# Wider DMA rows, a new order of the output stores and a new placement of the zero stores in a decode forward-and-backward kernel

## The chip, the cores and the metric

The kernel runs on one core of one Trainium2 chip. The metric is the device time of one launch in microseconds. It was measured five times for the kernel before, and one further execution was profiled. All engine names are those of the profile: PE is the matrix engine, DVE and ACT are the two engines that copy results out of PSUM, POOL and SP issue transfers (SP does nothing else).

## The reference

A single token passes through four residual layers, attention (A1), MLP (B2), attention (A3), MLP (B4), and the kernel returns the output and the gradients of everything. The two attentions share their weights and caches, and so do the two MLPs, so every weight gradient is a sum over two layers.

```python
x = x + A(layernorm(x), k_cache, v_cache, wq, wo)   # 32 heads over 4 KV heads, last 4096 of 32768 positions
x = x + B(layernorm(x), w1, b1, w2)                 # h*tanh(softplus(h)), width 3584
x = x + A(layernorm(x), k_cache, v_cache, wq, wo)
x = x + B(layernorm(x), w1, b1, w2)
# results: x, and the vjp with grad_out for x, k_cache, v_cache, wq, wo, w1, b1, w2
```

All tensors are bfloat16 and D is 1024. The gradients of k_cache and v_cache have all 32768 positions, of which the first 28672 are zero. These zeros alone are 58.7 MB of the 98.8 MB that the kernel writes. The weight gradients are outer products of one column with one row per layer, so they cost almost no arithmetic and a lot of copying and storing.

## The kernel before

**Order of the work.** The program is one straight sequence: A1 forward (`attn_fwd`), B2 forward (`mlp_fwd`), A3 forward, then `mlp_turn`, which does B4 forward and the W1 part of its backward in seven blocks of 512 columns, then A3 backward (`attn_bwd`), the second pass over W2 (`W2Pass.rest`, which serves B4's forward and B2's backward), `mlp_bwd_w1` for B2, A1 backward, and at last a list of `jobs` that makes and stores the weight gradients. K, V, wq and ten of sixteen pieces of wo stay in the core's memory. The rest of wo, W1 and W2 stream through six slots (`strm`, `NB = 6`), so a load is issued by SP when the piece six before it has been used up.

**Loads.** SP first loads K (four transfers of 1 MB), wq (sixteen of 512 KB, lines 444 to 446: eight row blocks `t`, two halves each, so 4 KB per partition), V, and wo. `w1_block` (line 705) loads a block of W1 for B4 as 1 KB rows.

**Zero stores.** There are 112 zero stores of 512 KB. `bg_zeros(n, after)` (line 134) lets POOL issue n of them once the tile `after` has been written: a tiny copy to `gate_t` waits for it. `zeros(n)` (line 128) lets SP issue them. The table `Z` (line 1143) says how many go where: `A3` in A3 forward, `B4[b]` ahead of the loads of B4's block b, `A3c` and `A3d` in A3 backward, `B4w` in the W2 pass, `W1` and `W1m` in `mlp_bwd_w1` (one for each listed i), `A1c` on POOL in A1 backward. `A1d=100` lets SP issue all that are left there: 27.

**Output jobs.** A job makes 2048 columns of a gradient (1792 for W1) in four PSUM banks, DVE and ACT copy 1024 each to the core's memory (`ev_out`), and SP stores them. `stage["w"]` holds 14 jobs for dW2 and 16 for dW1 (`dw_wide`), `stage["v"]` 8 for dV and `stage["k"]` 8 for dK (`dkv`), `stage["o"]` 16 for dWo and `stage["q"]` 16 for dWq. Jobs of w, o and q store 512 KB each (dW1 448 KB) from slots of a rotating list. The dV and dK jobs fill the memory of `kv["K"]` and store twice, after jobs 3 and 7, in 4 KB rows. `weave(a, b)` puts one job of b after every two of a. The order is 14 dW2, then dW1 with dV, then dWo with dK, then dWq. Ten small preparation jobs (`late_prep`: layouts for later jobs) are put in at every fourth place from the fifth on. After the jobs nothing is left but the stores in flight.

Of the kernel before, what the change touches and what calls it, by code (L numbers as in the profile page):

```python
# [14 lines left out]
P = 128  # L15
HQ = 32
DH = 128
G = 4
# [5 lines left out]
def kernel(  # L24
# [22 lines left out]
    nc = tc.nc  # L47
# [5 lines left out]
    J = A_wq.shape[1]  # L53
# [11 lines left out]
    NW2 = TF // 2  # L65
# [19 lines left out]
    wq_v = A_wq.rearrange("(t p) j -> p t j", p=P)  # L85
# [48 lines left out]
    def bg_zeros(n, after):  # L134

        if n:
            nc.gpsimd.tensor_copy(gate_t[:], after[:, 0:1])
        for _ in range(min(n, len(zero_jobs))):
            nc.gpsimd.dma_start(zero_jobs.pop(0), zt[:])  # L139
# [18 lines left out]
    def shaped(t, shape):  # L158
        n = 1
        for k in shape[1:]:  # L160
            n *= k
        ap = t[0:shape[0], 0:n]
        if len(shape) == 3:
            return ap.rearrange("p (a b) -> p a b", a=shape[1])
        if len(shape) == 4:
            return ap.rearrange("p (a b c) -> p a b c", a=shape[1], b=shape[2])
        return ap
# [63 lines left out]
    def mm(out_ap, lhsT, rhs, start, stop, **kw):  # L231
        nc.tensor.matmul(out_ap, lhsT=lhsT, rhs=rhs, start=start, stop=stop, skip_group_check=True, **kw)  # L232
# [48 lines left out]
    def level():  # L281
        ev[:] = [0.0, 0.0]
# [50 lines left out]
    wq_b = keep.tile([P, TD, 2, J // 2], BF16, name="wq_b")  # L333
    wq_t = [wq_b[:, t, hf, :] for t in range(TD) for hf in range(2)]
# [4 lines left out]
    def load_kv(pool, nm, src):  # L339
        kv[nm] = pool.tile([P, G, TK, DH], BF16, name=nm)  # L340
        for g in range(G):
            nc.sync.dma_start(kv[nm][:, g, :, :], src[g])

    def kv_units(nm):
        for g in range(G):
            f = kv[nm][:, g, :, :].rearrange("p t d -> p (t d)")
            for k in range(4):
                yield f[:, k * 1024:(k + 1) * 1024]

    def wo_load(c):  # L350
        if c < NR:
            w = wo_kept[c]
        else:
            w = strm.tile([P, 2, D], BF16, name="wo_c", tag="st")[:]
        nc.sync.dma_start(w, wo_v[c])
        return w
# [30 lines left out]
    def pipe(items, T, M, lag=1):  # L387
        n = len(items)
        for i in range(n + lag):
            if i < n:  # L390
                T(items[i])
            if i >= lag:
                M(items[i - lag], i - lag)

    area = {}
# [44 lines left out]
    def attn_fwd(x_col, lname, first):  # L440
        if first:
            load_kv(keep, "K", k_v)
            ku = list(kv_units("K"))
            for t in range(TD):
                for hf in range(2):
                    nc.sync.dma_start(wq_t[2 * t + hf], wq_v[:, t, hf * (J // 2):(hf + 1) * (J // 2)])
            load_kv(keep, "V", v_v)
            for c in range(NR):
                wo_load(c)
# [22 lines left out]
        if not first:  # L472
            for c in range(NR, min(NO, NR + NB)):
                held[c] = wo_load(c)
            bg_zeros(Z["A3"], n_bf)
            for w in wq_t:
# [74 lines left out]
        for i, c in enumerate(order):  # L551
            if c not in held and c not in early:
                held[c] = wo_load(c)
            w = wo_kept[c] if c < NR else held.pop(c)
# [113 lines left out]
    def mlp_fwd(x_col, lname, g_bf):  # L668
# [5 lines left out]
        for i in range(2 * TD):  # L674
            t, hf = i // 2, i % 2
            w = w1_load(i)
            if i == 0:
                bg_zeros(Z["B2a"], x_col)
            if i == 4:
# [17 lines left out]
        sv["dact"] = dact  # L697
        x_new, wg = w2.rest(0, g_bf, x_col, f"x_{lname}", gbc, Z["B2"], last)
        return x_new, sv, wg
# [5 lines left out]
    def w1_block(b, hh):  # L705
        w = strm.tile([P, HT, CB], BF16, name="w1_b", tag="st")
        nc.sync.dma_start(w[:], w1_v[:, hh * HT:(hh + 1) * HT, b * CB:(b + 1) * CB])
        return w

    def mlp_turn(x_col, lname, wg, g_col, nxt):  # L710
# [22 lines left out]
        def lo0(b):  # L733
            return max(b - 1, 0) * FB
# [6 lines left out]
        for b in range(NBK):  # L741
            bg_zeros(Z["B4"][b], dh_bf[:, lo0(b):] if b else n_bf)
            ws[b] = [w1_block(b, hh) for hh in range(2)]
# [38 lines left out]
    def mlp_bwd_w1(g_col, lname, sv, nxt):  # L782
# [3 lines left out]
        def T(i):  # L786
            w = w1_load(i)
            ws[i] = w
            if i in Z["W1m"]:
                bg_zeros(1, ws[i - 1])  # L790
# [9 lines left out]
        level()  # L800
        bg_zeros(Z["W1"], sv["dh_bf"])
        pipe(list(range(2 * TD)), T, M)
# [229 lines left out]
    def stage_tile(shape):  # L1032
        s = slots.pop(0)
        slots.append(s)
        return shaped(s, shape)

    def ev_out(out_ap, in_ap, f=1.0):
        evac(out_ap, in_ap, 1.22 * f, 1.05 * f)

    def outer(lhsT, rhs, q, ps):  # L1040
        mm(ps, lhsT, rhs, True, True, tile_position=(32 * q, 0))

    jobs = []
# [5 lines left out]
    def out_banks():  # L1049

        if "pair" in pools:
            ts = [pools["pair"].tile([P, 1024], FP32, name="ops", tag="pair") for _ in range(2)]
            return [t[:, k * 512:(k + 1) * 512] for t in ts for k in range(2)], [(0, 2, ts[0][:]), (2, 2, ts[1][:])]
        bs = [psum1([P, 512], FP32, "ops") for _ in range(4)]
        return bs, [(k, 1, bs[k]) for k in range(4)]
# [13 lines left out]

        jobs.extend([lambda c=c: chunk(c) for c in range(nblk // 2)])  # L1070

    def dw_wide(R, last, step, perm, out_t):

        def chunk(t, hf):
            st = stage_tile([P, 2048])
            bs, gs = out_banks()
            for q in (0, 1, 2, 3):
                n = 512 if q < 3 else last
                outer(R()[32 * q:32 * q + 2, 0, t * P:(t + 1) * P], R()[32 * q:32 * q + 2, 1, hf * 512:hf * 512 + n], q, bs[q][:, 0:n])
            for k, n, ap in gs:  # L1080
                w = min(n * 512, step - k * 512)
                o, i = st[:, k * 512:k * 512 + w], ap[:, 0:w]
                if perm:
                    o, i = o.rearrange("p (c x t) -> p c t x", x=P, t=2), i.rearrange("p (c t x) -> p c t x", x=P, t=2)
                ev_out(o, i, w / 1024)
            nc.sync.dma_start(out_t[t * P:(t + 1) * P, hf * step:(hf + 1) * step], st[:, 0:step])

        jobs.extend([lambda t=t, hf=hf: chunk(t, hf) for t in range(TD) for hf in range(2)])

    def dkv(x3, y3, x1, y1, out_t):  # L1090
        ov = out_t[0, :, Sk - W:, :].rearrange("g (p t) d -> p g t d", p=P)

        def chunk(j):
            st = kv["K"]
            bs, gs = out_banks()
            for lay, (x, y) in enumerate(((x3, y3), (x1, y1))):
                for c in range(NC):
                    mm(bs[c], x[32 * c:32 * c + 32, j * P:(j + 1) * P],
                       y[32 * c:32 * c + 32, :, :].rearrange("p g d -> p (g d)"), lay == 0, lay == 1, tile_position=(32 * c, 0))
            for k, n, ap in gs:  # L1100
                t0 = 4 * j + k
                ev_out(st[:, :, t0:t0 + n, :].rearrange("p g t d -> p t g d"), ap.rearrange("p (t g d) -> p t g d", t=n, g=G), n / 2)
            if j % 4 == 3:
                for g in range(0, G, 2):
                    hs = slice(4 * j - 12, 4 * j + 4)
                    nc.sync.dma_start(ov[:, g:g + 2, hs, :], st[:, g:g + 2, hs, :])

        jobs.extend([lambda j=j: chunk(j) for j in range(TJ)])

# [30 lines left out]
        for _ in range(min(n, len(prep))):  # L1140
            prep.pop(0)()

    Z = dict(B2a=1, B2={0: 1, 4: 1, NW2 - 2: 3}, A3=16, B4=[4, 2, 2, 2, 2, 2, 5], A3c=6, A3d=27, B4w={1: 1, 4: 1, 7: 1, 10: 1}, W1=2, W1m=(5, 10), A1c=3, A1d=100)


    x1 = None
# [35 lines left out]
    x1, sA1 = attn_fwd(x0, "A1", True)  # L1182
    x2, sB2, wg4 = mlp_fwd(x1, "B2", gcolb)
    x3, sA3 = attn_fwd(x2, "A3", False)
# [46 lines left out]
    def r3(nm):  # L1231
        return area[nm].rearrange("p (g d) -> p g d", g=G)

    slots.extend(wq_t)
    stage = {}

    def take(nm):
# [1 line left out]
        del jobs[:]  # L1239

    take("w")
    dkv(area["p3"], r3("do3"), sA1["p"], r3("do1"), out_3)
    take("v")
    dw_tall("wo", HQ, out_5.rearrange("(c p t) d -> c p t d", p=P, t=2))
    take("o")
    dkv(sA3["ds"], r3("q3"), sA1["ds"], r3("q1"), out_2)
    take("k")
    dw_wide(lambda: area["Rq"], 512, 2048, False, out_4)
    take("q")
    late_prep = [  # L1250
        lambda: row_layout(sA3["dorep"], "do3"),
        lambda: row_layout(sA1["dorep"], "do1"),
        lambda: tall_left("wo", "o", 0),
        lambda: tall_left("wo", "o", 1),
        lambda: tall_right("wo", "gA"),
        lambda: row_layout(sA3["qrep"], "q3"),
        lambda: row_layout(sA1["qrep"], "q1"),
        lambda: rows_put(area["Rq"], 0, "nA", "rep"),
# [1 line left out]
        db1_out,  # L1260
    ]

    def weave(a, b):
        while a or b:
            jobs.extend(a[0:2])
            jobs.extend(b[0:1])
            del a[0:2], b[0:1]

    n2 = NW2
    jobs.extend(stage["w"][:n2])  # L1270
    weave(stage["w"][n2:], stage["v"])
    weave(stage["o"], stage["k"])
    jobs.extend(stage["q"])
    for k, f in enumerate(late_prep):
        jobs.insert(5 + 4 * k, f)
    run(1000)
    zeros(1000)
    assert not zero_jobs
# [30 lines left out]
```

## Time and profile before

| what | value |
|---|---|
| median of five runs | 447.18 us (443.79 to 449.1) |
| the profiled execution, whole | 445.38 us |
| its span | 443.6 us |
| bytes moved | 171.18 MB, mean 386 GB/s |
| packets | 52048, of which 1076 of 8 KB or more |
| busy: PE, DVE, ACT, POOL | 73%, 54%, 50%, 14% |
| zero stores: on POOL, on SP | 85, 27 |

The profiled execution took 1.8 us less than the median. Of its 445.38 us, 1.78 lie outside the span. The busy shares of the engines are means over stages that differ a lot. The share that is even over the whole span is that of the transfers, so this page is read from its DMA rows, and then stage by stage.

### The profile page before, as it was taken

The numbers are of one execution on the slowest core, as the hardware profiler recorded it, in microseconds if no ns is written. First come the engines' busy times: TensorE is split into PE (matmuls) and PEld (weight loads), VectorE is DVE, ScalarE is ACT, GpSimd is POOL, SyncE is SP. The second block draws the span as 40 slices with busy tenths as digits, with TensorE's granted clock in tenths as the row PEclk, the third lists the DMA queues.
The fourth block names the chain that finished last, engine by engine and source line by source line (L and its number), as shares of the span: only waits on it lengthen the run. The fifth ranks groups of instructions, "written<-read, shape, count | busy, mean of one in ns | idle before, by whom it ended". The sixth has DMA issues, their size and how long they took to land.

```text
span 443.6 us, 11728 instructions
## 1 busy us (share of the span) xinstructions
PE 323.4 (73%) x5004; PEld 218.4 (49%) x5004; DVE 240.6 (54%) x492; ACT 220.8 (50%) x256; POOL 63.9 (14%) x165
## 2 busy tenths in 40 slices
PE   1466756498988699887899588878966777888930
PEld 0233515397376699775596577856422212122100
DVE  2134201196343367665374664465359788999950
ACT  1121200065144377766693354435037777998940
POOL 2000000011332122242142112014010100000000
PEclk9998655575888889989999758998975555555555
DMA  8999999999999989999999999999999969899997
GB/s 317 377 413 418 406 409 385 409 384 378 392 415 380 395 298 369 402 410 387 417 414 407 353 383 348 381 400 414 417 417 407 417 253 396 331 406 405 404 405 315
DMA packets 52048, 171.18 MB, mean 386 GB/s; under 512 B 5184, under 2 KB 12380, under 8 KB 50972
## 3 DMA queue, kind: packets, MB, share of 16 engines
q1 hardware_dynamic: 39536, 125.58, 73.0%
q0 software_dynamic: 12416, 44.84, 25.6%
q8 instruction: 39, 0.64, 0.6%
q14 instruction: 13, 0.11, 0.1%
q10 hardware_dynamic: 44, 0.01, 0.0%
HBM read 71.58 MB, written 98.84 MB: 384 GB/s over the span
## 4 chain that ended last, share of the span: by engine, by line
PE 22%; ACT 13%; DMA 7%; DVE 6%; issue 3%; POOL 1%; DVEq 0%; ACTq 0%; SPq 0%
DMA w_c<-in_B_w_dram 7%; PE tps L196 6%; PE ops L232 5%; ACT wq_b L149 5%; PE acc L232 4%; ACT K L149 2%; PE sm L232 2%; ACT wo_b L149 2%; ACT st_o L149 2%; ACT V L149 2%; PE rw L983 2%; DVE K L146 1%; PE d L232 1%; PE tps L630 1%; DVE st_o L146 1%
## 5 line engine op out<-in xcount | busy, mean ns | idle before, releaser
L139 POOL DMA_DIRECT2D out_dram<-zt x85 | 45.5, 538 | 42.4 <-DMA out_dram<-zt 37.3
L232 PEld LDWEIGHTS <-w_c 128*128 128x128 bf16 x1120 | 37.4, 102 | 23.3 <-DMA w_c<-in_B_w_dram 17.6
L640 ACT COPY w_c<-tps 128x1024 bf16<-128x1024 bf16 x28 | 28.3, 1012 | 28.6 <-PE tps L630 20.9
L654 DVE CUSTOM_DVE_ANT_0 scr<-w_c,gbc 128x1024 bf16<-128x1024 bf16 x28 | 34.2, 1221 | 10.6 <-DMA w_c<-in_B_w_dram 9.3
L232 PE MATMUL ops<-V 2*128 2x512 bf16 (+1 forms) x160 | 34.2, 600 | 5.0 <-DVE K L146 2.7
L232 PEld LDWEIGHTS <-V 128*128 128x128 bf16 (+2 forms) x448 | 17.1, 102 | 37.5 <-issue 37.2
L149 ACT CAST wq_b<-ops 128x1024 bf16<-128x1024 f32 (+1 forms) x32 | 33.4, 1120 | 3.8 <-PE ops L232 3.4
L149 ACT COPY K<-tps 128x1024 bf16<-128x1024 bf16 x20 | 19.6, 1021 | 29.6 <-PE tps L196 29.5
L146 DVE CAST wq_b<-ops 128x1024 bf16<-128x1024 f32 (+1 forms) x28 | 30.5, 1144 | 1.1 <-PE ops L232 1.0
L232 PE MATMUL ops<-wo_b 2*128 2x512 bf16 x120 | 23.7, 571 | 8.0 <-ACT wo_b L149 2.3
L630 PE MATMUL tps<-ident_bf,w_c 128*128 128x128 bf16 x224 | 23.9, 273 | 0.7 <-DMA w_c<-in_B_w_dram 0.7
L232 PE MATMUL q<-wq_b,nA_pair 128*32 128x512 bf16 x128 | 10.8, 418 | 16.8 <-DMA wq_b<-in_A_wq_dram 16.8
L146 DVE CAST K<-ops 128x1024 bf16<-128x1024 f32 x16 | 19.6, 1224 | 6.2 <-PE ops L232 6.1
L149 ACT COPY w_b<-tps 128x1024 bf16<-128x1024 bf16 x20 | 19.5, 1015 | 6.1 <-PE tps L196 4.7
L232 PE MATMUL acc<-a_pair,w_c 128*128 128x16 bf16 x448 | 15.9, 173 | 8.4 <-DMA w_c<-in_B_w_dram 8.3
L146 DVE COPY K<-tps 128x1024 bf16<-128x1024 bf16 x12 | 8.1, 690 | 25.5 <-PE tps L196 23.6
L248 DVE COPY yr<-acc 128x512 f32<-128x512 f32 x6 | 4.2, 692 | 30.2 <-PE acc L232 30.2
L196 PE MATMUL tps<-ident_bf,K 128*128 128x128 bf16 x256 | 19.3, 235 | 0.0
L196 PE MATMUL tps<-ident_bf,w_c 128*128 128x128 bf16 x224 | 16.5, 231 | 3.1 <-DMA w_c<-in_B_w_dram 2.9
L630 PEld LDWEIGHTS <-w_c 128*128 128x128 bf16 x224 | 18.1, 123 | 1.2 <-DMA w_c<-in_B_w_dram 0.8
L149 ACT CAST K<-ops 128x1024 bf16<-128x1024 f32 x16 | 16.2, 1012 | 5.1 <-PE ops L232 5.0
L149 ACT COPY w_c<-tps 128x768 bf16<-128x768 bf16 (+1 forms) x14 | 11.6, 830 | 14.0 <-PE tps L196 14.0
(326 smaller groups left out, 655.5 us busy)
## 6 DMA issues: line engine op xcount, KB each, us to landing
out_dram<-zt POOLq DMA_DIRECT2D x85, 512.0 KB, 10.2
w_c<-in_B_w_dram SPq DMA_DIRECT2D x32, 448.0 KB, 6.3
w_c<-in_B_w_dram SPq DMA_DIRECT2D x28, 512.0 KB, 7.1
out_dram<-zt SPq DMA_DIRECT2D x27, 512.0 KB, 10.1
wo_c<-in_A_wo_dram SPq DMA_DIRECT2D x24, 512.0 KB, 7.3
wq_b<-in_A_wq_dram SPq DMA_DIRECT2D x16, 512.0 KB, 11.5
out_dram<-K SPq DMA_DIRECT2D x8, 1024.0 KB, 7.8
out_dram<-wq_b SPq DMA_DIRECT2D x16, 512.0 KB, 9.7
```

The source lines that it names most:

```text
L139: nc.gpsimd.dma_start(zero_jobs.pop(0), zt[:])
L146: nc.vector.tensor_copy(out_ap, in_ap)
L149: nc.scalar.copy(out_ap, in_ap)
L196: nc.tensor.transpose(ps[:, b, :], ap, ident_bf[:])
L232: nc.tensor.matmul(out_ap, lhsT=lhsT, rhs=rhs, start=start, stop=stop, skip_group_check=True, **kw)
L248: nc.vector.tensor_copy(yr[:], bank[:])
L630: nc.tensor.transpose(self.ps[c][:, b, :], w[:, 1, b * P:(b + 1) * P], ident_bf[:])
L640: nc.scalar.copy(self.w[c][:, 1, :], self.ps.pop(c)[:].rearrange("p b c -> p (b c)"))
L654: nc.vector.tensor_tensor_reduce(out=scr[:], in0=w[:, 0, :], in1=gbc[:], scale=1.0, scalar=0.0, op0=ALU.mult, op1=ALU.add, accum_out=self. ...
L983: nc.tensor.transpose(ps[:, j, :], sp[:, j, :], ident_bf[:])
```

## The change

The load of wq becomes eight transfers of 1 MB with 8 KB per partition. dWq is no longer staged in rotating slots: both halves of a row block are written to that block's place in `wq_b` and are stored together, as 1 MB with 8 KB rows. dV and dK are stored once, after their last job, one group per transfer, 1 MB each with 8 KB rows (the argument `half` is False in both calls).

The order of the jobs becomes 14 dW2, 8 dW1, then one dV job after each of the other 8 dW1, then all 16 dWo, then dWq with a dK job after every two. So dV's stores follow the last dV job, and dK's stores are the last of all. The preparation jobs get places of their own.

In `Z`, A3 goes from 16 to 14, B4's first entry from 4 to 0, A3d from 27 to 28, and W1m from two places to four. That is 82 zero stores on POOL for 85, and 30 on SP in A1 backward for 27.

```diff
             for t in range(TD):
-                for hf in range(2):
-                    nc.sync.dma_start(wq_t[2 * t + hf], wq_v[:, t, hf * (J // 2):(hf + 1) * (J // 2)])
+                nc.sync.dma_start(wq_b[:, t, :, :].rearrange("p h j -> p (h j)"), wq_v[:, t, :])
...
-    def dw_wide(R, last, step, perm, out_t):
+    def dw_wide(R, last, step, perm, out_t, home=None):
...
-            st = stage_tile([P, 2048])
+            st = stage_tile([P, 2048]) if home is None else home[2 * t + hf]
...
-            nc.sync.dma_start(out_t[t * P:(t + 1) * P, hf * step:(hf + 1) * step], st[:, 0:step])
+            if home is None:
+                nc.sync.dma_start(out_t[t * P:(t + 1) * P, hf * step:(hf + 1) * step], st[:, 0:step])
+            elif hf:
+                nc.sync.dma_start(out_t[t * P:(t + 1) * P, :], wq_b[:, t, :, :].rearrange("p h j -> p (h j)"))
...
-    def dkv(x3, y3, x1, y1, out_t):
+    def dkv(x3, y3, x1, y1, out_t, half):
...
-            if j % 4 == 3:
-                for g in range(0, G, 2):
-                    hs = slice(4 * j - 12, 4 * j + 4)
-                    nc.sync.dma_start(ov[:, g:g + 2, hs, :], st[:, g:g + 2, hs, :])
+            if j % 4 == 3 and (j > 4 or half):
+                hs = slice(4 * j - 12 if half else 0, 4 * j + 4)
+                for g in range(G):
+                    nc.sync.dma_start(ov[:, g, hs, :], st[:, g, hs, :])
...
-    Z = dict(B2a=1, B2={0: 1, 4: 1, NW2 - 2: 3}, A3=16, B4=[4, 2, 2, 2, 2, 2, 5], A3c=6, A3d=27, B4w={1: 1, 4: 1, 7: 1, 10: 1}, W1=2, W1m=(5, 10), A1c=3, A1d=100)
+    Z = dict(B2a=1, B2={0: 1, 4: 1, NW2 - 2: 3}, A3=14, B4=[0, 2, 2, 2, 2, 2, 5], A3c=6, A3d=28, B4w={1: 1, 4: 1, 7: 1, 10: 1}, W1=2, W1m=(3, 6, 9, 12), A1c=3, A1d=100)
...
-    dw_wide(lambda: area["Rq"], 512, 2048, False, out_4)
+    dw_wide(lambda: area["Rq"], 512, 2048, False, out_4, wq_t)
...
-    n2 = NW2
-    jobs.extend(stage["w"][:n2])
-    weave(stage["w"][n2:], stage["v"])
-    weave(stage["o"], stage["k"])
-    jobs.extend(stage["q"])
-    for k, f in enumerate(late_prep):
-        jobs.insert(5 + 4 * k, f)
+    jobs.extend(stage["w"][:NW2 + 8])
+    weave(stage["w"][NW2 + 8:], stage["v"], 1)
+    jobs.extend(stage["o"])
+    weave(stage["q"], stage["k"], 2)
+    for at, f in zip((8, 11, 24, 27, 30, 40, 43, 46, 49, 51), late_prep):
+        jobs.insert(at, f)
```

More of the change, by code (lines that the diff above doesn't have):

```diff
@@ L1241 @@
     take("w")
-    dkv(area["p3"], r3("do3"), sA1["p"], r3("do1"), out_3)
+    dkv(area["p3"], r3("do3"), sA1["p"], r3("do1"), out_3, False)
     take("v")
@@ L1245 @@
     take("o")
-    dkv(sA3["ds"], r3("q3"), sA1["ds"], r3("q1"), out_2)
+    dkv(sA3["ds"], r3("q3"), sA1["ds"], r3("q1"), out_2, False)
     take("k")
-    dw_wide(lambda: area["Rq"], 512, 2048, False, out_4)
+    dw_wide(lambda: area["Rq"], 512, 2048, False, out_4, wq_t)
     take("q")
@@ L1261, with weave @@
     ]
-    def weave(a, b):
+    def weave(a, b, n):
         while a or b:
-            jobs.extend(a[0:2])
+            jobs.extend(a[0:n])
             jobs.extend(b[0:1])
-            del a[0:2], b[0:1]
-    n2 = NW2
-    jobs.extend(stage["w"][:n2])
-    weave(stage["w"][n2:], stage["v"])
-    weave(stage["o"], stage["k"])
-    jobs.extend(stage["q"])
-    for k, f in enumerate(late_prep):
-        jobs.insert(5 + 4 * k, f)
+            del a[0:n], b[0:1]
+    jobs.extend(stage["w"][:NW2 + 8])
[4 more added lines that the diff above has]
+        jobs.insert(at, f)
     run(1000)
```

## The prediction

> **What bounds the kernel now.** I read the page's slices first, then the span cut into windows by stage, then the timelines of PE, ACT and SP in the stages that the change touches, and last the chain of waits.
>
> ```profile
> DMA  8999999999999989999999999999999969899997
> GB/s 317 377 413 418 406 409 385 409 384 378 392 415 380 395 298 369 402 410 387 417 414 407 353 383 348 381 400 414 417 417 407 417 253 396 331 406 405 404 405 315
> ```
>
> The transfer engines are busy nearly everywhere. So bytes only moved to another place gain nothing by themselves. A gain must come from idle transfer time, from a faster transfer of the same bytes, or from a stage where something waits for a load behind a zero store. The windows give the first two (columns: busy us of PE, PEld, DVE, ACT, POOL with counts, then PE clock, DMA share, GB/s):
>
> ```profile
> 4.00:12.00 8.00, 0.76 (x5) 0.65 (x6) 1.91 (x12) 0.50 (x2) 0.00 (x0) 1.00 1.01 426
> 16.00:32.00 16.00, 10.85 (x140) 7.03 (x136) 4.06 (x6) 4.05 (x4) 0.00 (x0) 1.00 1.03 408
> 32.00:44.00 12.00, 7.56 (x97) 3.90 (x94) 4.99 (x9) 2.72 (x4) 0.00 (x0) 0.86 1.02 419
> ...
> 349.60:383.10 33.50, 25.14 (x158) 6.60 (x158) 27.50 (x37) 27.59 (x27) 1.17 (x5) 0.50 0.83 332
> 383.10:390.00 6.90, 6.47 (x34) 1.40 (x34) 6.84 (x6) 6.13 (x7) 0.00 (x0) 0.50 1.00 390
> 390.00:412.00 22.00, 17.92 (x103) 4.51 (x102) 20.39 (x19) 20.11 (x22) 0.00 (x0) 0.50 1.02 406
> 412.00:426.00 14.00, 12.02 (x54) 2.50 (x51) 14.00 (x13) 13.57 (x16) 0.00 (x0) 0.50 1.02 404
> 426.00:441.00 15.00, 0.00 (x0) 0.00 (x0) 1.25 (x2) 0.70 (x1) 0.00 (x0) 0.50 1.02 406
> ```
>
> The first row is mainly K (8 KB rows), the second wq (4 KB), the third mainly V (8 KB): the larger rows move 419 to 426 GB/s, the smaller 408. From 349.6 to 383.1, the stage of dW1 with dV, the transfers are idle 17% of 33.5 us: 5.7 us. After that they are full to the end, and from 426 on nothing else works: the end is when the stores are through.
>
> The third is B4 (PE's timeline: start, busy, tiles, and in brackets the idle before and what ended it):
>
> ```profile
> 143.30 0.19 PE L232 MATMUL sm<-b_b,ident_bf 128*128 128x64 bf16 x1
> 143.94 0.56 PE L232 MATMUL sm<-nB_pair,w_b 128*128 128x16 bf16 x16 [0.45 <-DMA w_b<-in_B_w_dram]
> 145.88 0.58 PE L232 MATMUL sm<-nB_pair,w_b 128*128 128x16 bf16 x16 [1.38 <-DMA w_b<-in_B_w_dram]
> ...
> 151.36 0.19 PE L232 MATMUL sm<-b_b,ident_bf 128*128 128x64 bf16 x1
> ...
> 154.12 0.56 PE L232 MATMUL sm<-nB_pair,w_b 128*128 128x16 bf16 x16 [2.18 <-DMA w_b<-in_B_w_dram]
> ...
> 160.54 0.19 PE L232 MATMUL sm<-b_b,ident_bf 128*128 128x64 bf16 x1
> ...
> 165.74 0.19 PE L232 MATMUL sm<-b_b,ident_bf 128*128 128x64 bf16 x1
> ```
>
> The product with b_b opens a block. Blocks 0 and 1 take 8.06 and 9.18 us, block 2 takes 5.20, and there PE never idles. The first two wait for W1.
>
> **The change part by part.** Every term is against the profiled execution: 445.38 us whole, 443.6 span, and 1.8 us under the median of 447.18. I add the sum to the median.
>
> *B4's first blocks, −6.8 us.* POOL's timeline has the sixteenth zero store of A3 at 132.03 us and the four of B4 at 142.38 to 144.5. A zero store lands 10.2 us after its issue (median), since about eight are in flight. SP issues the first W1 blocks at 133.48, behind these: the first lands at 143.9 and the fourth, which block 1 needs, at 154.1, though such a load can land in 4.1 us (the least in its tile's row; the longest is 17.1). Two zero stores less in A3 and four less here are 6 × 524 KB = 3.1 MB, 7.5 us at 417 GB/s. The first four blocks (2.1 MB, 5.8 us at the 364 GB/s of block 3's window) are then in by about 145, and block 1 starts at 148.5. So both blocks can take 5.20: 17.24 − 10.40 = 6.8. PE was also at 0.79 and 0.81 of full clock in these two, at 1.00 in block 2, so the stall's end restores the clock too. Later blocks have two zero stores each as before, and block 2 to 4 wait for no load with them. What else could bound: the start at 143.3 comes from the layer norm and V's transposes, which don't change. Bounds: 0 (the loads are slow by their 1 KB rows, whatever runs beside them) and −6.8; I take −6.8, since blocks 2 to 4 load the same rows beside two zero stores each without a wait. What is late next are the copies of DVE and ACT (8.1 of 10.4 busy us in block 2), not far behind.
>
> *wq in 8 KB rows, −0.7 us.* 8.39 MB take 20.6 us at 408 GB/s, and 19.9 at 421. The stage is bound by transfers until 65 us (PE waits 0.66 us before each of the last wo pieces), so it counts in full. The first row block now needs 1 MB instead of 512 KB, 1.2 us later, and eight products of 0.39 us follow the last load instead of four, 1.6 us later for the scores of A1. Behind these stands the wait for wo at 55 to 65 us, 0.65 us before each of nine pieces, which takes it up: PE has only 24 products to do before 55 and would do them later. If it didn't, +1.6.
>
> *One zero store more in A3d, +1.2 us.* The 27 keep POOL's queue full until 238.6 and land until about 249. The first W2 load that is waited for (243.25 to 250.1 in the chain below) lands behind them. One more is 524 KB at 410. POOL's own next work is a gate at 244.5, after 5.4 us of idling, so nothing queues on POOL.
>
> *Two more in W1m, +2.1 us.* Here PE waits for W1 loads:
>
> ```profile
> 243.25 6.85 DMA w_c<-in_B_w_dram
> ...
> 251.91 10.04 DMA w_c<-in_B_w_dram
> ...
> 276.70 6.92 DMA w_c<-in_B_w_dram
> ...
> 285.10 5.69 DMA w_c<-in_B_w_dram
> ```
>
> Two stores are 2.6 us at 410; the DMA share is 0.95, 0.92 and 0.98 in 264 to 273, so some 0.5 us go into gaps. The gates (four copies of 0.19 us on POOL) wait for the copies of the piece before; nothing is queued behind them before 294. Bounds 0.5 and 2.6.
>
> *Three more on SP, and the output jobs, +0.3 us.* SP issues its zero stores from 293.6 to 329.3 and then, in order, the load of p3 and the jobs' stores. Three more hold it 3.8 us longer. p3 then lands at about 343 and is needed at 357. The stores of dW2 wait in 32 slots of 512 KB, which were never short. So these 3.8 us only lengthen the backlog, which is what fills the gap of 349 to 383. For the end I need t, the time at which the stage of dW1 and dV ends, because before and after it the stores are bound from there on. Job times: dWq alone 14.0 us for 16, 0.88 each. dWo, dWo, dK repeats every 3.48 us (ACT's copies to K at 388.34 and 409.20, six periods), so a dK or dV job is 1.7. dW1 is then 0.98 (its share of the 33.5 us: 16 × 0.98 + 8 × 1.7 + 7 preparations × 0.6 = 33.5, and the 0.6 of DVE and ACT time fits their rows). Before, t is 383.1. After: dW2 ends at 349.0 (one preparation less), eight dW1 at 356.8, eight pairs of 2.68 at 378.2, four preparations at 380.7. From t on remain all of dV, dK and dWq, 16.78 MB in 8 KB rows, 40.0 us at 420, and dWo, 8.39 MB at 406, 20.7 us: 441.4. Before it was 441.1. The delay of dV's first half (2.1 MB, 5 us) and the faster rows and fewer preparations cancel. dK's four stores come at the end with 10 us left; before, 15 us of stores were left there, so this tail hides behind what is queued anyway. The copies for dWq go straight to wq_b, with no instruction more; its slots were last read by dW1's stores 40 us earlier. kv["K"] is written again by dK's first copy at about 399 (t, 16 dWo, four or five preparations, two dWq), and dV's stores have passed by 391, so this wait costs nothing unless they are 8 us late.
>
> Here two rules of the Trainium skill, in "DMA: Bandwidth & Descriptors", speak on the row size. Section "Anatomy of one DMA" gives, for POOL's path, about 2.0 us fixed per transfer plus the bytes: 16 transfers fewer would be 32 us if each stood alone. The wq loads follow each other every 1.28 us (524 KB at 408), under that cost, so it is hidden and I count 0. Section "SWDGE vs HWDGE vs iDMA" says a packet is at most 4096 B preferably. By it 8 KB rows gain nothing: the wq term goes, dV, dK and dWq take 41.3 us at 406 instead of 40.0, and the sum is 2.0 us worse. The three windows above (426 and 419 against 408) are loads, and no 8 KB store is in this trace; I follow the windows.
>
> Sum: −6.8 − 0.7 + 1.2 + 2.1 + 0.3 = −3.9. 445.38 becomes 441.5, and the median 447.18 becomes 443.3.
>
> **The rivals.**
> *A: as summed,* 443.3, chance 0.50. By its bounds it runs from 440 to 446.5.
> *B: the output phase gains too,* chance 0.25. If the pairs are limited only by the copies (3840 columns at 1.1 us per 1024 on two engines, 2.1 us), t is 4.6 us earlier, and the transfers drop from then on: 438.7. For it: DVE and ACT are only 82% busy in 349 to 383. Against it: a dV job fills both PSUM pairs, and PE then idles for ACT.
> *C: B4 hardly gains,* chance 0.13. If 1 KB rows limit the loads, −2 instead of −6.8: 448. For it: this stage never exceeds 411 GB/s and falls to 300 with a share of 0.87. Against it: blocks 2 to 4.
> *D: the pairs starve the stores, slower,* chance 0.12. If in dW1–dV PE and the copies don't overlap, a pair costs 0.61 + 1.75 (PE's times for dW1 and for dV) + 1.23 (DVE's copy) = 3.6 us. t is then 388.1 and the end 7.4 us later: 450.7, and above 451.7 (1%) if W1m costs its full 2.6 and wq's later scores 1.6. It decides from 3.17 us a pair on, where the gain of 3.9 is used up. For it: the two PSUM pairs alternate between the two kinds, so a dV product waits for the last dV copy. Against it: 3.48 for three jobs with the same product.
> That the change doesn't do what it says is excluded by the diff but for the row size: one row per packet is what the 1076 packets of 8 KB show for K and V.
>
> **How the numbers follow.** 1% of 447.18 is 4.5 us, which is also about what a measurement of this kernel can tell from none: under 442.7 is faster, over 451.7 slower. A is at 443.3, and 0.4 of its 0.50 lies below; with B's 0.25 faster has 0.45. Slower takes most of D, with a little of C: 0.12. The rest is 0.43. The range leaves out the best of B and the worst of D: 437 to 450.5; A alone has 440 to 446.5.
>
> **What would show it.** B4: blocks 0 and 1 at 5.2 to 5.6 us and the clock at 1.00 in them; if they stay above 7, the first step is wrong. Loads of wq at 415 GB/s or more. In the W2 pass and the W1 stage, DMA waits longer by 1 and 2 us. In the output phase t at 381 plus the shift of the stages before (−4), the store rate above 412 GB/s in the last 40 us, and the copies done about 10 to 12 us before the stores. The prediction is wrong if the dW1–dV pairs take over 3 us, if 8 KB stores move no faster than 406 GB/s, or if A1's forward gets longer by wq's later products.

## The result, and the profile after

The changed kernel takes 443.72 us (median of 24 runs, 439.38 to 449.48), the kernel before 447.41 us (median of 43), 3.7 us more. The ratio is 0.9899 with a 95% interval of 0.988 to 0.9919: 1.0% less, or 4.5 us. The ratios leave out executions more than 1.5% above the fastest of their kernel, here 5 of 24 and 2 of 43, which is why 3.7 and 4.5 us differ; the traces of e9_b4_back and e12_b4_later are of such executions, so no difference in length rests on them. The profiled execution of the changed kernel has a span of 439.8 us, 3.8 us under that of before.

Both traces can be cut at the same places: at the instruction that writes a layer's normalised input (line 302) and at the one that writes a gradient leaving a layer (line 326). All times in us.

| stretch | before | after | difference | predicted |
|---|---|---|---|---|
| start to B2's input (A1 forward) | 70.4 | 69.0 | −1.4 | −0.7 |
| to A3's input (B2 forward) | 42.9 | 42.7 | −0.2 | 0 |
| to B4's input (A3 forward) | 28.2 | 27.9 | −0.3 | 0 |
| to B4's gradient | 51.3 | 46.1 | −5.2 | −6.8 |
| to A3's gradient | 47.3 | 48.2 | +0.9 | +1.2, here and in the next row |
| to B2's gradient (W2 pass, W1 stage) | 54.8 | 57.4 | +2.6 | +2.1 |
| to A1's gradient | 32.8 | 32.2 | −0.6 | 0 |
| to the end (output stage) | 116.0 | 116.4 | +0.4 | +0.3 |

The page's slices after, with the packet line:

```profile
DMA  7999999999999999999999999999999998999997
GB/s 317 424 419 415 408 408 392 406 368 358 399 416 373 308 339 330 379 414 416 416 409 387 384 392 358 358 392 414 417 416 414 419 408 359 375 403 406 419 422 313
DMA packets 48720, 171.18 MB, mean 389 GB/s; under 512 B 4928, under 2 KB 12124, under 8 KB 44572
```

The same bytes go in 3328 packets less, 4148 of them now of 8 KB or more (1076 before). In the output stage a slice of 253 GB/s was the thinnest but the last, now it is one of 359, and two of the last slices run at 419 and 422 for 404 and 405. In exchange the slices of B4 move less together (308, 339 and 330 for 395, 298 and 369).

B4 on PE's timeline. The product with b_b opens a block, and the bracket has PE's idle time and what ended it:

```profile
141.38 0.19 PE L232 MATMUL sm<-b_b,ident_bf 128*128 128x64 bf16 x1
...
142.29 0.56 PE L232 MATMUL sm<-nB_pair,w_b 128*128 128x16 bf16 x16 [0.33 <-DMA w_b<-in_B_w_dram]
...
146.27 0.19 PE L232 MATMUL sm<-b_b,ident_bf 128*128 128x64 bf16 x1
...
151.48 0.19 PE L232 MATMUL sm<-b_b,ident_bf 128*128 128x64 bf16 x1
...
156.92 0.19 PE L232 MATMUL sm<-b_b,ident_bf 128*128 128x64 bf16 x1
...
160.34 1.61 PE L196 MATMUL tps<-ident_bf,wo_b 128*128 128x128 bf16 x26
164.20 0.51 PE L196 MATMUL tps<-ident_bf,wo_b 128*128 128x128 bf16 x6 [2.25 <-issue]
164.55 0.19 PE L232 MATMUL sm<-b_b,ident_bf 128*128 128x64 bf16 x1
```

Blocks 0 and 1 take 4.89 and 5.21 us (8.06 and 9.18 before); the waits for W1 have shrunk to 0.33, and the clock granted to PE in the two blocks is 1.00 (0.79 and 0.81 before). But block 3 now takes 7.63 us (5.20 before): PE stops for 2.25 us after 26 of 32 transposes, and "issue" says that it waited for no data that the profile shows. So a part of what was won went to a new stall. What ended it is in the last section.

The chain of waits after, in the W2 pass and the W1 stage:

```profile
238.32 9.80 DMA w_c<-in_B_w_dram
...
249.90 7.92 DMA w_c<-in_B_w_dram
...
270.56 8.69 DMA w_c<-in_B_w_dram
...
280.74 5.45 DMA w_c<-in_B_w_dram
```

The four waits are 31.9 us together, 29.5 before: these stages are as bound by loads as they were, and the added zero stores show there.

The output stage in windows (busy us of PE, PEld, DVE, ACT, POOL, then PE clock, DMA share, GB/s):

```profile
345.60:375.30 29.70, 23.87 (x152) 7.33 (x151) 25.95 (x33) 24.66 (x24) 1.90 (x10) 0.50 0.97 387
375.30:390.00 14.70, 10.68 (x65) 3.19 (x64) 13.37 (x15) 13.21 (x15) 0.52 (x1) 0.50 0.96 389
...
412.00:427.00 15.00, 8.35 (x44) 1.59 (x43) 9.09 (x8) 9.21 (x10) 0.00 (x0) 0.50 1.01 418
```

The stage of dW1 and dV ends at 375.3 (dV's first store). Its transfers idle 3% of the time now instead of 17%, yet the output stage as a whole is no shorter. First before, then after:

```profile
327.60:443.60 116.00, 76.08 (x431) 19.44 (x431) 89.55 (x98) 84.15 (x85) 4.01 (x20) 0.50 0.94 376
323.40:439.80 116.40, 75.57 (x431) 19.64 (x431) 89.22 (x98) 84.49 (x85) 4.12 (x20) 0.50 0.98 395
```

It moves more in the same time: 376 GB/s over 116.0 us are 43.6 MB, 395 over 116.4 are 46.0 MB. Of the 2.4 MB more, 1.6 are the three zero stores that were taken from earlier stages.

### The profile page after: what moved, and what is told of

It is laid out like the page before. It is cut to its first block, busy times and chain, and to the rows that moved or that the text cites. A ratio compares the mean times of both kernels' runs of the same rounds, so it can differ in the third digit from the quotient of the medians.

```text
span 439.8 us, 11711 instructions
## 1 busy us (share of the span) xinstructions
PE 320.0 (73%) x5004; PEld 215.2 (49%) x5004; DVE 240.1 (55%) x492; ACT 221.0 (50%) x256; POOL 62.5 (14%) x163
## 4 chain that ended last, share of the span: by engine, by line
PE 23%; ACT 14%; DMA 9%; DVE 4%; issue 2%; POOL 1%; ACTq 0%; SPq 0%; DVEq 0%
DMA w_c<-in_B_w_dram 7%; PE ops L232 6%; PE tps L196 6%; PE acc L232 5%; ACT wq_b L149 4%; ACT K L149 4%; ACT st_o L149 2%; DMA out_dram<-st_o 2%; PE sm L232 2%; ACT V L149 1%; ACT wo_b L149 1%; PE rw L982 1%; PE d L232 1%; PE tps L629 1%; PE wps L155 1%
## 5 line engine op out<-in xcount | busy, mean ns | idle before, releaser
L139 POOL DMA_DIRECT2D out_dram<-zt x82 | 43.8, 537 | 43.4 <-DMA out_dram<-zt 38.0
L232 PEld LDWEIGHTS <-w_c 128*128 128x128 bf16 x1120 | 37.4, 102 | 24.7 <-DMA w_c<-in_B_w_dram 18.9
L149 ACT CAST wq_b<-ops 128x1024 bf16<-128x1024 f32 (+1 forms) x33 | 35.8, 1127 | 1.9 <-PE ops L232 1.8
L146 DVE CAST wq_b<-ops 128x1024 bf16<-128x1024 f32 (+1 forms) x31 | 34.4, 1138 | 2.2 <-PE ops L232 1.8
L232 PEld LDWEIGHTS <-V 128*128 128x128 bf16 (+2 forms) x448 | 16.9, 102 | 34.4 <-issue 32.8
L232 PE MATMUL q<-wq_b,nA_pair 128*32 128x512 bf16 x128 | 9.6, 418 | 15.8 <-DMA wq_b<-in_A_wq_dram 15.8
L232 PEld LDWEIGHTS <-wo_b 2*128 2x128 bf16 (+1 forms) x184 | 7.5, 99 | 27.2 <-issue 25.0
L149 ACT CAST K<-ops 128x1024 bf16<-128x1024 f32 x17 | 17.1, 1012 | 6.5 <-PE ops L232 6.2
L146 DVE CAST K<-ops 128x1024 bf16<-128x1024 f32 x15 | 18.3, 1221 | 3.1 <-PE ops L232 2.7
L146 DVE COPY w_c<-tps 128x1024 bf16<-128x1024 bf16 (+1 forms) x18 | 11.7, 661 | 13.3 <-PE tps L196 10.9
```

The source lines that it names most:

```text
L146: nc.vector.tensor_copy(out_ap, in_ap)
L149: nc.scalar.copy(out_ap, in_ap)
```

## The experiments

The question was which of the parts carries the 4.5 us, and why the output stage, with less idle time and faster rows, is no shorter. Each kernel was timed against the kernel before on the same chip. Most ratios are known to about 0.35%, so the difference of two of them to about 0.5%, or 2 us. Where one trace is compared with another, mind how much they vary: up to A1's gradient e2_outputs issues the same work as the kernel before, and from A3's input to B4's gradient it took 76.2 us where the trace of before has 79.5, with its wait for W1 in block 2 instead of 0 and 1. So the ratios decide and the traces tell where.

**Parts of the change alone.**

e1_b4_zeros: the kernel before, with

```diff
-A3=16, B4=[4, 2, 2, 2, 2, 2, 5]
+A3=14, B4=[0, 2, 2, 2, 2, 2, 5]
```

> The kernel before with only A3=14 and B4's first entry 0; the six zero stores taken away go to the end of SP's list (33 instead of 27). Theory (the zero stores ahead of B4's loads cost waits): blocks 0 and 1 of B4 take 4.9 and 5.2 us as in the changed kernel (before 8.1 and 9.2), the gradient that leaves B4 comes 5 to 6 us earlier (192.8 before), nothing changes up to the end of A1's backward, and in the output stage the six stores (7.5 us) fill the idle 5.7 us and overrun it by about 2: total -3.5 us. Rival (transfers are busy everywhere, a zero store moved is a zero store paid elsewhere): B4 is shorter but the output stage is longer by the same 5 to 7.5 us: total 0 to +2 us.

Measured: 0.9916 (0.9881 to 0.9951), −3.8 us. PE has no wait for W1 in B4, blocks 0 and 1 take 4.4 and 5.2 us, and B4's gradient is out at 190.2. The output stage takes 117.3 us with 33 zero stores, and its gap is closed:

```profile
345.00:385.00 40.00, 30.83 (x192) 8.16 (x190) 33.92 (x42) 33.13 (x33) 1.77 (x7) 0.50 1.02 408
```

Theory right in the total, and its rival is out. The gradient came only 2.6 us earlier in this trace, since A3 took 0.8 us more and the stall in block 3 is here too (1.68 us).

e8_before_z: the kernel before with the new table `Z`.

> The kernel before with the whole new table of zero stores and nothing else. Theory: B4 gives 5.3 us, the W2 pass and the W1 stage take 3 to 3.7 back, the three more stores on SP fill idle time of the dW1-dV stage: total -1.5 to -3 us. Rival: all of the change's 3.8 us comes from rows and order, and this alone is 0.

Measured: 0.9956 (0.9923 to 0.9988), −2.0 us. From B4's to B2's gradient it takes 108.6 us (102.1 before, 102.6 in e1_b4_zeros). The additions to A3d and W1m give back about half of what B4 wins. The difference to e1_b4_zeros, 0.4%, lies within the two intervals. What speaks for it is the stretch: 102.1 to 104.7 us in the three traces with the old numbers in A3d and W1m (before, e1_b4_zeros, e2_outputs), 105.7 to 108.6 in the seven with the new ones.

e2_outputs: the changed kernel with the old table and the old loads of wq.

> The changed kernel with the old table of zero stores and the old wq loads, so that only the new order and rows of the output stores remain. Theory (they cancel): up to the last gradient (327.6 us before) as before, and the output stage within 1 us of before: total 0 +-1 us. Rival (8 KB rows at 420 GB/s and no gap in the dW1-dV stage): output stage 3 to 4 us shorter, total -3 to -4 us.

Measured: 0.9986 (0.9954 to 1.0017), no difference. Output stage 116.6 us, before 116.0. Its window of dW1 and dV:

```profile
350.00:382.00 32.00, 24.91 (x158) 7.38 (x158) 27.91 (x34) 26.97 (x26) 1.75 (x10) 0.50 0.74 298
```

With the new order the transfers idle 26% here, 8.3 us, more than in the order of before (5.7): dV's first half is held back. The total is the same, so what the rows and the order win elsewhere makes up for it, as the theory had it.

e3_wq_4k: the changed kernel with the old loads of wq.

```diff
-                nc.sync.dma_start(wq_b[:, t, :, :].rearrange("p h j -> p (h j)"), wq_v[:, t, :])
+                for hf in range(2):
+                    nc.sync.dma_start(wq_t[2 * t + hf], wq_v[:, t, hf * (J // 2):(hf + 1) * (J // 2)])
```

> The changed kernel with wq loaded as sixteen transfers with 4 KB rows again. Theory: 408 GB/s instead of 422 in 16 to 32 us, A1 ends 0.7 to 1.4 us later, and because the stage is bound by its loads the whole kernel too: +0.7 to +1.4 us on the changed kernel. Rival (what is saved at the start is taken back by zero stores that land later): A1 later by 1 us, total 0.

Measured: 0.994 (0.9908 to 0.9971), some 1.8 us slower than the changed kernel, a little more than expected, with intervals that just overlap. B2's input comes at 70.3 us; in the five kernels with 4 KB rows it comes at 70.2 to 70.6, in the nine with 8 KB rows at 68.9 to 69.5. The 1.3 us are more than the rate alone makes. The rest is at the seam, where the loads of wq follow those of K. First the kernel before, then the changed kernel (e3_wq_4k has 347 GB/s there):

```profile
12.00:16.00 4.00, 0.53 (x4) 0.11 (x4) 0.00 (x0) 0.00 (x0) 0.00 (x0) 1.00 0.95 329
```

```profile
12.00:16.00 4.00, 0.00 (x0) 0.00 (x0) 0.00 (x0) 0.00 (x0) 0.00 (x0) 1.00 1.01 422
```

The three parts, −2.0, −0.6 and −1.8 us, add up to 4.4 of the 4.5 us measured, but each is known to some 1.5 us only.

e9_b4_back: the changed kernel with A3=16 and B4's first entry 4 again.

> The changed kernel with A3=16 and B4's first entry 4 again (so 24 zero stores are left for SP instead of 30). Theory: PE waits for W1 blocks in B4 come back (9.6 us summed over PE's two rows and the copies in the kernel before, 6.0 in e2_outputs, 0.7 in the changed kernel), the way from A3's layer norm to the gradient of B4 is 2 to 5 us longer than in the changed kernel (73.9), the dW1-dV stage has 7 us less zero stores to fill it and idles more: total 2.5 to 5 us slower than the changed kernel, near the kernel before. Rival (the stall of 1.7 to 2.5 us in B4's block 3 that the runs without the four stores show, with PE waiting for no data, replaces the wait): 0 to 1.5 us slower.

Measured: 1.0019 (0.9987 to 1.0052), 5.4 us slower than the changed kernel, a little more than expected, and no better than before. With the six zero stores back ahead of B4's loads, nothing is left of the gain. The rival, that the stall in block 3 merely replaces the wait, is out as to the size.

**Why the output stage is no shorter.**

e4_halves: the changed kernel with dV and dK stored in two halves (`dkv(..., True)` in both calls).

> The changed kernel with dV and dK stored in two halves each (half True: after jobs 3 and 7, 4 KB rows). Theory: dV's first half fills the transfers' idle time before t (8.3 us in e2_outputs, about 2 in the changed kernel), the slower rows cost 8.4 MB x (1/406 - 1/418) = 0.6 us, dK's early half shortens the last tail by nothing as the transfers are full then: 0 to 1.5 us faster than the changed kernel. Rival (8 KB rows are what the output side gains): 1 us slower or more.

Measured: 0.9866 (0.9821 to 0.9911). The output stage takes 113.2 us instead of 116.4. First the changed kernel's window, then that of e4_halves:

```profile
345.00:375.00 30.00, 23.69 (x152) 7.03 (x149) 26.12 (x32) 24.95 (x24) 1.90 (x10) 0.50 0.98 391
375.00:380.00 5.00, 3.55 (x28) 1.74 (x26) 4.25 (x5) 4.63 (x6) 0.00 (x0) 0.50 0.84 344
```

```profile
345.00:375.00 30.00, 22.98 (x146) 6.56 (x142) 25.45 (x29) 26.09 (x24) 1.89 (x10) 0.50 1.02 410
375.00:380.00 5.00, 4.02 (x28) 1.50 (x27) 4.91 (x8) 3.69 (x5) 0.00 (x0) 0.50 1.02 404
```

Now there is no gap. e10_dv_halves stores only dV in halves.

> The changed kernel with dV stored in two halves (4 KB rows), dK whole. Theory (what e4_halves won, 3.2 us of output stage, 113.2 for 116.4, is dV's first half stored before the transfers run dry): output stage 113 to 114 us, no idle transfer time before t, 1 to 3 us faster than the changed kernel, as e4_halves. Rival (it was dK's half, which shortens the last tail): as the changed kernel.

Measured: 0.9871 (0.9833 to 0.9909), output stage 112.8 us, and no gap either (410 and 404 GB/s in the same two windows). So dV's first half is enough to close the gap, as the theory said, and dK's isn't needed.

The gap's worth is less than the 3.2 and 3.6 us by which the output stage is shorter. A1's backward, just before it, took 33.3 and 35.1 us in these two traces for 32.2, with the transfers full (shares of 1.02 and 1.03), so more zero stores were out when the output stage began: it moved 45.1 MB (398 GB/s) and 44.7 MB (396) for 46.0 (395). From B2's gradient to the end the two take 146.4 and 147.9 us, the changed kernel 148.6. Both ratios are ahead of the changed kernel's 0.9899 by 0.3%, within the intervals. These are the lowest ratios of the study, but a gain over the changed kernel of 1 to 2 us is likely and not shown.

e11_halves_w1m: e4_halves with `W1m=()`. e6_w1m: the changed kernel with `W1m=()`.

> e4_halves with no zero stores in the middle of the W1 stage (34 on SP). Theory (with dV in halves the transfers have no idle time left in the output stage, so a moved zero store is paid there): W1 stage 4 us shorter, output stage 4 to 5 us longer than e4_halves' 113.2: total as e4_halves, 0 +-1 us. Rival (gains add): 2 to 4 us faster than e4_halves.

> The changed kernel with no zero stores in the middle of the W1 stage (W1m empty; 34 for SP). Theory (each costs there what it moves, 1.28 us, as PE waits for loads): from B2's dh to the gradient that leaves the stage 3.5 to 5 us less; the output stage, whose length was 116.0, 115.8 and 117.3 us with 27, 30 and 33 stores on SP, is 1.5 to 3 us longer than in the changed kernel: total 1 to 3 us faster than the changed kernel. Rival (moved is paid elsewhere): 0.

Measured: e11_halves_w1m 0.9908 (0.9877 to 0.9938), 1.9 us slower than e4_halves where 0 ± 1 was expected, with intervals that overlap. W2 pass and W1 stage take 57.1 us for the 58.6 of e4_halves, the output stage 120.1 us for 113.2. From B2's gradient to the end it is 152.2 us for 146.4, at the same 401 GB/s. The four moved stores are 2.1 MB, 5.2 us at this rate: with no gap left, a moved zero store is paid in full at the end.

e6_w1m 0.9897 (0.9858 to 0.9935): the changed kernel's time, a miss for its theory. W2 pass and W1 stage are shorter as expected (53.5 for 57.4), and the output stage is as long as in the changed kernel with 34 zero stores for 30 (116.5). But A1's backward took 35.1 us for 32.2, and zero stores went out during it, so the two have to be taken together. From B2's gradient to the end, first the changed kernel, then e6_w1m:

```profile
291.25:439.83 148.58, 101.30 (x828) 35.41 (x826) 105.39 (x136) 94.20 (x98) 11.42 (x47) 0.60 0.99 400
290.11:441.74 151.63, 104.91 (x828) 38.28 (x826) 105.42 (x136) 94.21 (x98) 11.20 (x47) 0.58 0.99 401
```

Of the 3.9 us won, 3.1 are paid here, with transfers as full as in the changed kernel: the rival, that what is moved is paid elsewhere, is what this trace shows. A3 and B4 forward took 2.6 us more in it as well, which the edit doesn't touch.

e5_old_order: the changed kernel with the order of before, the wide rows kept.

```diff
-    jobs.extend(stage["w"][:NW2 + 8])
-    weave(stage["w"][NW2 + 8:], stage["v"], 1)
-    jobs.extend(stage["o"])
-    weave(stage["q"], stage["k"], 2)
+    jobs.extend(stage["w"][:n2])
+    weave(stage["w"][n2:], stage["v"])
+    weave(stage["o"], stage["k"])
+    jobs.extend(stage["q"])
```

> The changed kernel with the old order of the jobs and the old places of the preparations (14 dW2, dW1 with dV two to one, dWo with dK two to one, dWq last), the wide rows kept. Theory: dK's first job now comes right after dV's stores are issued and writes the memory that they read, so its copies wait 8 to 10 us for these stores, PE and the dWo jobs behind them wait too; the transfers have dV's 10 us to do meanwhile and then run dry: 4 to 8 us slower than the changed kernel. Rival (slots and backlog absorb it): within 1 us.

Measured: 1.0174 (1.0132 to 1.0216), 12 us slower than the changed kernel, more than expected. The copies of dK's first job wait for dV's stores:

```profile
395.09 1.01 ACT L149 CAST K<-ops 128x1024 bf16<-128x1024 f32 x1 [11.90 <-DMA out_dram<-K]
395.11 1.23 DVE L146 CAST K<-ops 128x1024 bf16<-128x1024 f32 x1 [11.38 <-DMA out_dram<-K]
...
396.15 0.84 PE L232 MATMUL ops<-V 2*128 2x512 bf16 x4 [11.76 <-ACT K L149]
```

All three engines stand still. Production then can't make up for it: the transfers are at a share of 0.67 to 0.76 from 390 to 420. So the new order is what the whole-tensor stores need. Whether it gains anything by itself, with the stores in halves, no run isolates.

**Two smaller questions.**

e13_wq_out_4k: the changed kernel with dWq stored per half, sixteen times 512 KB.

> The changed kernel with dWq stored per half again, sixteen transfers of 512 KB in 4 KB rows from the same place. Theory: the last 25 us of stores run at 404 to 410 instead of 414 to 418 GB/s, but the halves are there 1 us earlier: 0 to 0.7 us slower than the changed kernel. Rival (row size does nothing for stores): same rate, 0 or a little faster.

Measured: 0.9939 (0.9905 to 0.9972), 1.8 us beyond the changed kernel's, more than expected, with intervals that just overlap. Its output stage takes 116.9 us, 0.5 more, which is what the rate makes of dWq's 8.4 MB; the rest of the 1.8 is not accounted for. The late stores, first in the changed kernel, then here:

```profile
415.00:430.00 15.00, 5.50 (x28) 1.02 (x25) 6.08 (x6) 6.37 (x7) 0.00 (x0) 0.50 1.01 421
415.00:430.00 15.00, 7.47 (x40) 1.46 (x37) 8.10 (x8) 8.24 (x9) 0.00 (x0) 0.50 1.02 407
```

So dWq's stores move about 3% faster in 8 KB rows. In this run, as in that of the wq loads, the transfers with 4 KB rows are also half as large (512 KB for 1 MB); which of the two makes the rate, no run separates.

e12_b4_later: the changed kernel with `B4=[0, 0, 0, 2, 2, 2, 5]`.

> The changed kernel with no zero stores ahead of B4's blocks 1 and 2 either (34 on SP). Theory (the stall of 1.7 to 2.5 us in block 3, in which no engine waits for data, comes from full transfer queues): it shrinks to under 1 us and the gradient of B4 comes 1 to 3 us earlier; the total is 0 to 2 us less, as 34 stores on SP cost the output stage nothing in e6_w1m. Rival (it has its place in the program, whatever the queues hold): the stall stays at 1.7 to 2.5 us and the total is unchanged.

Measured: 0.9907 (0.9869 to 0.9946), the changed kernel's time. Block 3 on PE:

```profile
163.73 1.95 PE L196 MATMUL tps<-ident_bf,wo_b 128*128 128x128 bf16 x32
```

The 32 transposes run through: the stall is gone, as the theory of full queues wants. The total doesn't show it. The four stores that were moved to the end have to be made there, and e11_halves_w1m showed what that costs, so this says nothing against the theory.

## Why the prediction was right

Predicted 443.3 us, measured 443.7, and the sum −3.9 against −3.8 in the span. The main step, that zero stores ahead of B4's loads cost time there, was right. That the sum fits so closely is partly luck: B4 gave 1.6 us less than taken, and 0.7 more in A1's forward and 1.1 in three stretches that were taken at 0 made up for it. The same instructions in those three vary by more than these differences from trace to trace (B2's forward from 42.4 to 44.1 us).

- **B4, −6.8:** right in mechanism, too large by 1.6. Blocks 0 and 1 gave 7.1 us, even a little more than taken, and the clock in them rose to 1.00. What was missed is what came late next: not the copies of DVE and ACT, as the step said, but a stall of 2.25 us in block 3, which is gone in e12_b4_later with the zero stores of blocks 1 and 2. By ratios the six stores are worth 3.8 us (e1_b4_zeros) to 5.4 us (e9_b4_back).
- **wq, −0.7:** measured −1.4, −1.3 over all kernels: half of it was missing. The rate was right (422 GB/s against the 421 taken). The slow seam from K to wq was in the trace of before at 329 GB/s and wasn't counted. The later products that it allowed for cost nothing: PE waits 0.66 us and more for the wo pieces as before.
- **A3d and W1m, +1.2 and +2.1:** measured +0.9 and +2.6 in the two stretches, 3.5 for 3.3. Over the ten traces named at e8_before_z the means differ by 3.8.
- **Output stage, +0.3:** measured +0.4. That three more zero stores on SP would only fill the gap was right: the stage moved 2.4 MB more in this time. Of the two opposite terms behind it, the held-back half of dV leaves the transfers idle for 8.3 us in e2_outputs, and 8 KB rows move 421 GB/s for 407 in e13_wq_out_4k; what each is worth in the end is within the noise. The stage of dW1 and dV ended at 375.3, the prediction had 380.7 less the 4.2 us by which everything came earlier, 376.5. A pair took 2.26 us (ACT's copies to K at 358.45 and 367.49, four periods) where 2.68 was taken. What followed took 62.0 us for 60.7, about 0.9 us of it because the transfers were not full in the first 5 us after (344 GB/s).
- **The choice on rows** between the Trainium skill's preference for packets of at most 4096 B ("DMA: Bandwidth & Descriptors", section "SWDGE vs HWDGE vs iDMA", where it stands with what POOL builds for its transfers; these are SP's) and the windows of this trace was rightly made for the windows: loads 422, stores 418 to 421 GB/s with 8 KB, 408 and 407 with 4 KB.
- **Rivals:** C and D are out (in B4 PE waits for no load of W1 over 0.33 us; pairs of 2.26 us). B's 2.1 us pairs nearly came true, and its gain in the end still did not: from the end of that stage on, only bytes and rate count.

## What to carry to other kernels

Where transfers are busy nearly all the time, moving background stores is not neutral: ahead of loads that a full engine waits for, six of them (7.5 us of transfer) cost 3.8 to 5.4 us here, and in front of a gap three cost nothing. With no gap left, four that were moved to the end cost 5.8 us there. Merging stores into larger ones has a price beside its rate: what is held back until it is whole can't fill the gap before, and a buffer that is stored whole is free only when all of it has landed. Before such a change, compute from the time at which the last gap closes: the rest is bytes over rate. And where transfers are full, compare stages by the bytes they moved and not by their length alone: a slow stage before lets more of the queue drain, and makes the next one look faster.

## What the runs showed of the hardware that was not expected

In the ten traces without the four stores ahead of B4 but with two each ahead of blocks 1 and 2, PE stops once in block 3, after 26 of 32 transposes, for 1.4 to 2.5 us. DVE and ACT wait for PE then, and PE for nothing that the profile names. But the traces do show what came: transfers of instructions are a queue of their own (q8, 39 packets of 16 KB). In the changed kernel PE stops at 161.95 us and goes on at 164.20, and the DMA view of 161.85 to 161.95 has

```profile
q8 instruction: 1, 0.02, 54.9%
```

This packet starts at 161.89 and takes 0.88 us. In all ten traces PE goes on 1.3 to 1.6 us after such a packet is through, which started 4.1 to 5.2 us into the block. In the four without the stop (before, e2_outputs, e9_b4_back, e12_b4_later) it started 1.4 to 2.1 us into it and was through before PE came to the place. The same holds everywhere: PE stops for over 0.6 us with the releaser "issue" 38 times in the fourteen traces, at 130 to 135 us in all of them and late in B4 in eight, and each stop ends 1.23 to 1.56 us after a packet of q8. These packets are some 8 us apart, so this is no chance: PE waits for instructions there. That the packet is late because of the zero stores is not shown: e12_b4_later, one trace, speaks for it, and no trace shows when a packet was asked for.

A1's backward, the same instructions in all kernels, took from 32.0 to 35.2 us, and its length goes with the clock granted over it. With a mean of 0.97 or 0.98 it took 32.0 to 32.2 us (four traces), with 0.94 or 0.95 it took 32.7 to 32.9 (three), with 0.91 it took 33.2 and 33.3, and with 0.84 or 0.85 it took 35.1 to 35.2 (e2_outputs, e6_w1m, e10_dv_halves). What lowers the clock is not shown. It does not go with the edits: e6_w1m and e11_halves_w1m, both with `W1m=()`, are at the two ends.

The first loads of 4 KB rows behind 8 KB rows ran at 322 to 347 GB/s for 4 us in all five kernels that have them; 8 KB rows behind 8 KB rows at 420 to 426 in the other nine.
